# First keys of a fused attention and ELU kernel: a PSUM tile for each turned quarter, and two loads that change queues

## The chip, the cores and the metric

The kernel runs on one core of one Trainium2 chip. The metric is the device time of one execution in microseconds (us). A core has TensorE (PE, matmuls; PEld is its weight load), VectorE (DVE), ScalarE (ACT), GpSimd (POOL) and SyncE (SP). SP and ACT both issue DMAs here, each on a queue of its own: q1 in the profile is SP's, q10 is ACT's. All times below are us, those of the trace from the start of the span.

## The reference

Attention with a threshold, for 8 batches of 8 heads, 576 rows and 64 columns per head, then a feed-forward block with ELU over the 4608 rows of 512:

```python
scores = q @ k.T / 8                      # per batch and head, 576 x 576
thresh = max(scores, axis=-1) - tau
scores = where(scores >= thresh, scores, -1e9)
attn = exp(scores - max) / (sum + 1e-9)
x = attn @ v                              # heads side by side: 4608 x 512
h = x @ w_in                              # 512 -> 2048
out = where(h > 0, h, exp(min(h, 0)) - 1) @ w_out    # 2048 -> 512
```

## The kernel before

Attention goes pair of heads by pair of heads (32 pairs, two heads on 2 x 64 partitions), each pair in five steps of 128 query rows (the last of 64). Of a pair's queries and keys the kernel keeps `qT` and `kT`, with the 64 columns of a head on partitions and rows along the free axis. The scores of a step (`scores`, L681) are four matmuls: for each of two heads two halves of 288 keys. VectorE takes the row maximum (L738), a threshold is made of it (L756 or L742), ScalarE and VectorE make the masked exponentials (L761, L767, L776, L783), the weights are normalised, turned on TensorE or by VectorE, and multiplied with `v`. The feed-forward block of a batch is woven in on TensorE as soon as its rows are there, with a scheme of seven products in place of eight for most of the work. The order of all instructions on each engine is written out when the program is built, by a list of tasks with due times (`task`, `MOVED`); engines then run their own lists and wait for each other by semaphores.

The change is in the first of these tasks, `start()` in `early_tasks`, which runs once. It brings in the first pair's keys and the first 128 query rows, and turns them with TensorE. Loads, in the order of issue: on SP the keys of head 0 (`kb[:, 0]`, L1341), the keys of head 1 (`kb[:, 1]`, L1343), tau (L1345), the second 128 query rows of both heads (`qb[:, 1]`, L1346); on ACT the first query rows (`qb[:, 0]`, L1342) and the last 64 keys of both heads (`ends`, L1344). Behind them SP issues the loads of the next pair (L546), whose keys use the same tile `km` that holds `kb`.

A partition of `kb` holds four rows of a head's keys: they lie in two blocks of 128 columns (`e`), and a block holds two rows of 64 (`o`). TensorE turns one block at a time by a transposing matmul against the identity (`turn_rows`, L1357), and gets a 128 x 128 tile: on its first 64 partitions the quarter `o = 0`, on the others `o = 1`. Before, both blocks of a head lie in one PSUM tile (`a` for head 0, `b` for head 1), and for each `o` one copy (L1374) of 64 partitions by 256 columns brings two quarters into `kT`, one `o` by VectorE and the other by ScalarE. `ends` are turned into `turned[:, 1]` and copied by VectorE twice: `kT[:, S:]` (L1377), the tail of head 0's keys, and `kT[D:, :TAIL]` (L1378), that of head 1's. Head 0's keys stand in columns 64 to 640 of `kT`, head 1's in columns 0 to 576.

Ahead of the turns TensorE multiplies a constant tile (L1364) and then turns the identity eight times, to no use of the result (`warm`, L800), and once more before the turn of `ends`. The first step's four score matmuls have the heads one after the other (`HEADS_APART`): head 0 first half, head 0 second half, head 1 first half, head 1 second half. Then come, on TensorE, the turn of the second query rows (`rest_of_first_q`), which ScalarE copies (L1383), and the scores of the second step.

PSUM tiles: `blank` and `turned` are the two tiles of the pool `t` (four slots of 128 columns each, 2 KB per partition), `a`, `b`, `c` the three of the pool `s` (two banks each). Before, `c` is allotted here and not used.

Of the kernel before, what the change touches and what calls it, by code (L numbers as in the profile page):

```python
# [368 lines left out]
def kernel(  # L369
# [10 lines left out]
    nc = tc.nc  # L380
    PSUM = bass.MemoryType.PSUM
    P = 128
    B, H, S, D = q.shape
    DM, DF = moe_w_in.shape
    NC = S // P
# [930 lines left out]
    def early_tasks():  # L1316
# [18 lines left out]
        def start():  # L1335
            tiles = raws[0] = {"km": raw.tile([P, S // T, T], FP32, name="km")}
            kb = tiles["km"].rearrange("p j d -> p (j d)")[:, :MAIN].rearrange("p (i e f) -> p i e f", i=2, e=2)
            qb = wstage.tile([P, 2, 2, D], FP32, name="qb", bufs=1)
            ends = tiles["ends"] = wstage.tile([TAIL, 2, D], FP32, name="ends", bufs=1)

            nc.sync.dma_start(kb[:, 0], long_rows("k", 0).rearrange("p (e o) d -> p e (o d)", o=2))  # L1341
            nc.scalar.dma_start(qb[:, 0], first_rows("q", 0))  # L1342
            nc.sync.dma_start(kb[:, 1], long_rows("k", 1).rearrange("p (e o) d -> p e (o d)", o=2))  # L1343
            nc.scalar.dma_start(ends, first_rows("k", NC, TAIL))  # L1344
            nc.sync.dma_start(tau_sb, tau.to_broadcast([P, 1]))  # L1345
            nc.sync.dma_start(qb[:, 1], first_rows("q", 1))  # L1346
            nc.scalar.activation(keep, keep, AF.Exp)
            blank, turned = (psum["t"].tile([P, NC, P], FP32, name="rt", tag="rt") for _ in range(2))
            a, b, c = (psum["s"].tile([P, 2, 512], FP32, name="sc") for _ in range(3))
            qT, kT = room_q(0), room_k(0)  # L1350

            def warm(n):
                for _ in range(n):
                    transpose(blank[:, 0], ident)

            def turn_rows(dst, src, n=P):
                nc.tensor.matmul(dst, src, ident[:n, :n], is_transpose=True, skip_group_check=True)  # L1357

            def flat(src):
                return src.rearrange("p i d -> p (i d)")  # L1360

            ones = nc.const_aps.tensor(1.0, [P, P])
            for x in range(2):
                nc.tensor.matmul(blank[:, x], ones, ones, start=True, stop=True)  # L1364
            warm(8)
            turn_rows(turned[:, 0], flat(qb[:, 0]))
            nc.vector.tensor_copy(qT[:, :P], turned[:, 0])
            main = kT[:, TAIL:S].rearrange("p (e o n) -> p o e n", e=2, o=2)
            for h, room in ((0, a), (1, b)):
                r = slice(h * D, (h + 1) * D)  # L1370
                for e in range(2):
                    turn_rows(room[:, 0, e * P : (e + 1) * P], kb[:, h, e])
                for o, copy in ((h, nc.vector.tensor_copy), (1 - h, nc.scalar.copy)):
                    copy(main[r, o], room[o * D : (o + 1) * D, 0, : 2 * P].rearrange("p (e n) -> p e n", e=2))  # L1374
            warm(1)
            turn_rows(turned[:, 1, :TAIL], flat(ends), TAIL)
            nc.vector.tensor_copy(kT[:, S:], turned[:, 1, :TAIL])  # L1377
            nc.vector.tensor_copy(kT[D:, :TAIL], turned[D:, 1, :TAIL])  # L1378

            def rest_of_first_q():  # L1380
                rt = psum["t"].tile([P, NC, P], FP32, name="rt", tag="rt")
                turn_rows(rt[:, 0], flat(qb[:, 1]))
                nc.scalar.copy(qT[:, P : 2 * P], rt[:, 0])  # L1383

            first_q.append(rest_of_first_q)
            read_tau()
# [1019 lines left out]
```

## Time and profile before

| | |
|---|---|
| median of 3 runs | 1256.07 us (1256.03 to 1256.32) |
| profiled execution | 1257.65 us |
| its span in the trace | 1255.8 us |
| busy: PE, DVE, POOL, ACT | 1244.7, 1040.4, 727.8, 636.2 us |
| moved by DMA | 245.74 MB, mean 196 GB/s |

How to read the rows: a timeline row gives the start, the time taken, the engine, the line of the kernel, the operation, and "out<-in"; in brackets how long the engine stood idle before and what ended that. Rows with "x4" are merged: start of the first, sum of the stretch. "SPq" and "ACTq" rows are issues of DMAs by these engines. A row of a DMA issue group ends with its size and the time from the start of its issue to its landing. A row of a queue gives its packets and bytes up to the end of the window. A row of the chain of waits gives the start, the time and the line that the end of the kernel hung on. The ends of matmuls are modelled; their starts are not.

### The profile page before, as it was taken

To read this page: it belongs to the slowest core of one execution; us is meant where nothing else is said; L and a number is where in the kernel's file an instruction comes from. 1 tells how busy PE (TensorE), PEld (TensorE's weight loads), DVE (VectorE), ACT (ScalarE), POOL (GpSimd) and SP (SyncE) were. 2 spreads that over 40 slices of the span, in tenths; PEclk is the share of its full clock that TensorE was granted. 3 is DMA by queue.
4 is the path that set the end of the run, shared out by engine and by line. 5 is a ranking of instruction groups with operands and counts; after the bars stand their busy time and mean duration, and the time that the engine had idled before them with its cause. 6 is when DMAs were issued, how large, how long until landed. Compare 5 with 4: busy or idle time off the path is not lost.

```text
span 1255.8 us, 21112 instructions
## 1 busy us (share of the span) xinstructions
PE 1244.7 (99%) x6596; PEld 956.9 (76%) x6596; DVE 1040.4 (83%) x2196; ACT 636.2 (51%) x1334; POOL 727.8 (58%) x1064
## 2 busy tenths in 40 slices
PE   8999999999999999999999999999999999999998
PEld 6675576477887787878778787878788887788887
DVE  7888777789798978998889889898889876776983
ACT  7899776664453526253534445352625353465330
POOL 5778655687575748676576747584767655122000
PEclk9999999999999999999999999999999999999999
DMA  7456788998889998898989997999889885000001
GB/s 149 146 171 184 172 244 235 257 269 217 228 240 255 247 246 233 225 259 226 263 206 253 235 232 230 259 251 244 229 228 268 221 242 174 20 1 1 1 34 34
DMA packets 322303, 245.74 MB, mean 196 GB/s; under 512 B 205456, under 2 KB 286736, under 8 KB 322192
## 3 DMA queue, kind: packets, MB, share of 16 engines
q1 hardware_dynamic: 321376, 243.78, 72.3%
q8 instruction: 52, 0.85, 0.3%
q10 hardware_dynamic: 816, 0.62, 0.2%
q14 instruction: 59, 0.48, 0.2%
HBM read 154.53 MB, written 89.78 MB: 195 GB/s over the span
## 4 chain that ended last, share of the span: by engine, by line
PE 91%; DVE 3%; DMA 2%; ACT 2%; issue 1%; SPq 1%; POOL 1%; DVEq 0%; ACTq 0%; POOLq 0%
PE f L1869 23%; PE f L1729 21%; PE sc L985 8%; PE sc L1058 7%; PE f L2332 7%; PE f L2257 5%; PE f L1110 4%; PE sc L681 3%; PE f L1162 3%; PE f L2270 2%; PE pv L938 2%; PE rt L800 2%; PE sc L1050 1%; DMA there<-x 1%; PE sc L1045 1%
## 5 line engine op out<-in xcount | busy, mean ns | idle before, releaser
L992 DVE TENSOR_REDUCE mx<-sc 128x1 f32<-128x576 f32 x207 | 148.3, 750 | 30.0 <-PE sc L985 26.1
L734 POOL TENSOR_SCALAR w<-w,rs 128x576 f32<-128x576 f32 x144 | 115.8, 813 | 69.6 <-DVE rs L797 69.5
L1012 ACT ACTIVATE w<-sc,mx 128x576 f32<-128x576 f32 x113 | 81.5, 740 | 115.6 <-DVE mx L992 98.7
L876 DVE STREAM_TRANSPOSE x<-w 128x512 f32<-128x512 f32 (+1 forms) x153 | 108.9, 744 | 12.9 <-POOL w L734 11.5
L1004 POOL TENSOR_SCALAR th<-mx,ntau 128x2 f32<-128x2 f32 (+1 forms) x114 | 33.8, 296 | 134.5 <-DVE mx L992 134.5
L985 PE MATMUL sc<-kT,qT 64*128 64x448 f32 (+4 forms) x736 | 103.1, 416 | 0.2 <-ACT xs L1074 0.2
L985 PEld LDWEIGHTS sc<-kT,qT 64*128 64x128 f32 x736 | 80.7, 186 | 25.2 <-issue 16.2
L1019 DVE SCALAR_TENSOR_TENSOR w<-sc,th,w 128x576 f32<-128x576 f32 x113 | 88.2, 810 | 9.4 <-ACT w L1012 9.2
L1729 PE MATMUL f<-xt,sw 128*128 128x256 f32 x384 | 93.4, 386 | 0.4 <-DVE g L1751 0.4
L1729 PE MATMUL f<-xt,w_in 128*128 128x256 f32 x384 | 92.3, 382 | 0.0
L1869 PE MATMUL f<-w_out,s 128*128 128x256 f32 x384 | 92.0, 382 | 0.1
L1869 PE MATMUL f<-w_out,g 128*128 128x256 f32 x384 | 92.0, 382 | 0.0
L1729 PE MATMUL f<-x,w_in 128*128 128x256 f32 x384 | 90.9, 379 | 0.1
L1869 PE MATMUL f<-t,s 128*128 128x256 f32 x384 | 90.8, 379 | 0.0
L734 POOL TENSOR_SCALAR e<-e,rs 128x576 f32<-128x576 f32 x91 | 67.1, 741 | 35.3 <-DVE rs L797 33.9
L1729 PEld LDWEIGHTS f<-xt,sw 128*128 128x128 f32 x384 | 69.5, 189 | 16.7 <-issue 5.4
L1729 PEld LDWEIGHTS f<-xt,w_in 128*128 128x128 f32 x384 | 71.7, 190 | 12.8 <-ACT w L1743 2.2
L1869 PEld LDWEIGHTS f<-w_out,g 128*128 128x128 f32 x384 | 72.0, 190 | 12.4 <-issue 3.1
L1869 PEld LDWEIGHTS f<-w_out,s 128*128 128x128 f32 x384 | 71.9, 190 | 12.4 <-issue 2.5
L1729 PEld LDWEIGHTS f<-x,w_in 128*128 128x128 f32 x384 | 72.8, 190 | 10.5 <-ACT s L1743 0.7
L1869 PEld LDWEIGHTS f<-t,s 128*128 128x128 f32 x384 | 72.8, 190 | 10.3 <-POOL s L1816 0.4
L1816 POOL TENSOR_TENSOR s<-g 128x256 f32<-128x256 f32 x96 | 74.9, 785 | 8.0 <-DVE g L1779 7.5
(330 smaller groups left out, 3106.3 us busy)
## 6 DMA issues: line engine op xcount, KB each, us to landing
there<-x SPq DMA_DIRECT2D x444, 144.0 KB, 3.5
wTb<-there SPq DMA_DIRECT2D x58, 576.0 KB, 6.4
wTa<-there SPq DMA_DIRECT2D x53, 576.0 KB, 4.8
sw<-win_sums SPq DMA_DIRECT2D x46, 384.0 KB, 4.5
t<-wout_sums SPq DMA_DIRECT2D x33, 512.0 KB, 6.2
qm<-in_q_dram SPq DMA_DIRECT2D x124, 72.0 KB, 4.9
wst<-in_moe_w_in_dram SPq DMA_DIRECT2D x16, 512.0 KB, 4.5
vm<-in_v_dram SPq DMA_DIRECT2D x64, 128.0 KB, 3.8
```

Source lines behind the costliest of these rows:

```text
L734: nc.gpsimd.tensor_scalar(wv, wv, st["rs"][:, h : h + 1], 1.0, ALU.mult, ALU.mult)
L876: nc.vector.transpose(x[:, :, c0 : c0 + nc_], src.rearrange("p (c g n) -> p g c n", c=nc_, n=T))
L985: on_banks(nc.tensor.matmul(o, qT[r, i * P : (i + 1) * P], kT[r, k0 : k0 + n], start=True, stop=True, skip_group_check=True), o)
L992: on_banks(nc.vector.tensor_reduce(st["mx"][:, h : h + 1], st["sc", h], axis=AX.XY if i == NC else AX.X, op=ALU.max, negate=True), st["sc" ...
L1012: on_banks(nc.scalar.activation(st["e", h], st["sc", h], AF.Exp, bias=st["mx"][:, h : h + 1]), st["sc", h])
L1019: on_banks(nc.vector.scalar_tensor_tensor(st["e", h], st["sc", h], st["th"][:, h : h + 1], st["e", h], ALU.is_ge, ALU.mult, accum_out=st[" ...
L1058: on_banks(nc.tensor.matmul(o, vm[:, h, c], parts[part][:, g0:g1, h * (NC + 1) + c], start=False, stop=(c == NC - 1), skip_group_check=Tru ...
L1729: nc.tensor.matmul(loc["banks"][place], left[:, j], right[:, j], start=(begins and j == 0), stop=(j == 1), skip_group_check=True)
L1816: engine.tensor_tensor(o, x, y, op)
L1869: nc.tensor.matmul(place(m), lhs, rhs, start=(begins and v == 0), stop=(v == RU - 1), skip_group_check=True)
L2257: nc.tensor.matmul(o, w.rearrange("p (j f) -> p j f", j=KJ)[:, j], m, start=(j == 0 and x == 0), stop=(j == KJ - 1 and x == 1), skip_group ...
L2332: nc.tensor.matmul(banks8[2 * i + x // 2], h[:, tok], w, start=(f == 0 and x != 1), stop=(f == NFT - 1 and x != 0), skip_group_check=True)
```

## The change

Three things change in `start()`. The loads of head 1's keys and of the last keys change places: the last keys are SP's second load, head 1's keys ACT's second. Each block of turned keys gets a PSUM tile of its own: head 0's blocks `a` and `b`, head 1's `c` and the second slot of `blank`. VectorE copies both quarters of block 0 and ScalarE both quarters of block 1, each quarter by a copy of 64 partitions by 128 columns. And the order on TensorE becomes: six turns of the identity, head 0's two blocks, the first query rows, one turn of the identity, head 1's two blocks, the last keys. On VectorE the two copies of head 0 come ahead of that of the queries, and those of head 1 ahead of the two copies of the last keys. The order of all that follows on every engine is the same as before.

```diff
             nc.sync.dma_start(kb[:, 0], long_rows("k", 0).rearrange("p (e o) d -> p e (o d)", o=2))
             nc.scalar.dma_start(qb[:, 0], first_rows("q", 0))
-            nc.sync.dma_start(kb[:, 1], long_rows("k", 1).rearrange("p (e o) d -> p e (o d)", o=2))
-            nc.scalar.dma_start(ends, first_rows("k", NC, TAIL))
+            nc.sync.dma_start(ends, first_rows("k", NC, TAIL))
+            nc.scalar.dma_start(kb[:, 1], long_rows("k", 1).rearrange("p (e o) d -> p e (o d)", o=2))
             nc.sync.dma_start(tau_sb, tau.to_broadcast([P, 1]))
             nc.sync.dma_start(qb[:, 1], first_rows("q", 1))
...
-            warm(8)
+            def turn_keys(h, rooms):
+                for e in range(2):
+                    turn_rows(rooms[e], kb[:, h, e])
+
+            def copy_keys(h, rooms):
+                for e, copy in ((0, nc.vector.tensor_copy), (1, nc.scalar.copy)):
+                    for o in range(2):
+                        k0 = TAIL + (2 * e + o) * P
+                        copy(kT[h * D : (h + 1) * D, k0 : k0 + P], rooms[e][o * D : (o + 1) * D])
+
+            warm(6)
+            sides = (a[:, 0, :P], b[:, 0, :P]), (c[:, 0, :P], blank[:, 1])
+            turn_keys(0, sides[0])
             turn_rows(turned[:, 0], flat(qb[:, 0]))
+            copy_keys(0, sides[0])
             nc.vector.tensor_copy(qT[:, :P], turned[:, 0])
-            main = kT[:, TAIL:S].rearrange("p (e o n) -> p o e n", e=2, o=2)
-            for h, room in ((0, a), (1, b)):
-                r = slice(h * D, (h + 1) * D)
-                for e in range(2):
-                    turn_rows(room[:, 0, e * P : (e + 1) * P], kb[:, h, e])
-                for o, copy in ((h, nc.vector.tensor_copy), (1 - h, nc.scalar.copy)):
-                    copy(main[r, o], room[o * D : (o + 1) * D, 0, : 2 * P].rearrange("p (e n) -> p e n", e=2))
             warm(1)
+            turn_keys(1, sides[1])
             turn_rows(turned[:, 1, :TAIL], flat(ends), TAIL)
+            copy_keys(1, sides[1])
             nc.vector.tensor_copy(kT[:, S:], turned[:, 1, :TAIL])
             nc.vector.tensor_copy(kT[D:, :TAIL], turned[D:, 1, :TAIL])
```

## The prediction

> **What bounds the kernel now.** I read the page first, then the chain of waits for the first 20 us, then the timeline of each engine up to 11 us, then the DMA issues and queues of the same stretch.
>
> ```profile
> span 1255.8 us, 21112 instructions
> PE 1244.7 (99%) x6596; PEld 956.9 (76%) x6596; DVE 1040.4 (83%) x2196; ACT 636.2 (51%) x1334; POOL 727.8 (58%) x1064
> PE 91%; DVE 3%; DMA 2%; ACT 2%; issue 1%; SPq 1%; POOL 1%; DVEq 0%; ACTq 0%; POOLq 0%
> ```
>
> TensorE holds 91% of the chain that ended last. Nothing after the start is edited, so what the edit can give is a shift of the start that all later work carries along. The size of that shift is decided before 9 us:
>
> ```profile
> 3.87 0.85 PE sc L1357 x4
> 5.23 1.38 PE sc L681 x4
> 6.64 0.77 DVE mx L738
> 7.78 0.67 DVE mx L738
> 8.79 0.02 ACT w L761
> ```
>
> The chain runs through the four key turns (L1357), the first scores (L681), the two row maxima of VectorE, and into ScalarE's softmax. I call the four score matmuls of the first tile S1, S2 (head 0, first and second half of the keys), S3, S4 (head 1). The handle for the sum is the start of the first maximum, 6.64, which needs S2, and ScalarE's two L761, which need the maxima and stand behind the copy of the next queries.
>
> ```profile
> 1.53 1.72 PEld L800 LDWEIGHTS rt<-ident 128*128 128x128 f32 x8
> 3.32 0.18 PEld L1357 LDWEIGHTS rt<-ident,qb 128*128 128x128 f32 x1
> 3.45 0.42 PE L1357 MATMUL rt<-ident,qb 128*128 128x128 f32 x1
> 3.66 1.06 PE L1357 MATMUL sc<-ident,km 128*128 128x128 f32 x4
> 4.87 0.37 PE L1357 MATMUL rt<-ident,ends 64*128 64x64 f32 x1
> 5.21 1.44 PEld L681 LDWEIGHTS sc<-x 64*128 64x128 f32 x8 [0.16 <-ACT x L1374]
> 7.04 0.33 PE L1357 MATMUL rt<-ident,qb 128*128 128x128 f32 x1
> 5.21 0.91 PE L681 MATMUL sc<-x 64*128 64x288 f32 x2
> 5.71 0.67 PE L681 MATMUL sc<-x 64*128 64x288 f32 x3
> 6.20 0.42 PE L681 MATMUL sc<-x 64*128 64x288 f32 x2
> ```
>
> The last three rows are from narrow windows: S1's two passes start at 5.21 and 5.71, half a microsecond apart, and S2's second pass starts at 6.20, so from 5.71 a pass takes (6.20 - 5.71) / 2 = 0.245. A turn of 128 columns takes (3.66 - 3.45) = 0.21 here.
>
> ```profile
> 3.91 0.29 DVE L1367 COPY x<-rt 128x128 f32<-128x128 f32 x1 [2.93 <-PE rt L1357]
> 4.33 0.42 DVE L1374 COPY x<-sc 64x256 f32<-64x256 f32 x1
> 4.78 0.43 DVE L1374 COPY x<-sc 64x256 f32<-64x256 f32 x1
> 5.27 0.23 DVE L1377 COPY x<-rt 128x64 f32<-128x64 f32 x1
> 5.53 0.23 DVE L1378 COPY x<-rt 64x64 f32<-64x64 f32 x1
> 4.79 0.82 ACT L1374 COPY x<-sc 64x256 f32<-64x256 f32 x2 [1.30 <-DVE x L1374]
> 7.41 0.27 ACT L1383 COPY x<-rt 128x128 f32<-128x128 f32 x1 [1.80 <-PE rt L1357]
> 7.82 1.80 ACT L761 ACTIVATE w<-sc,th,keep 128x576 f32<-128x576 f32 x2
> 6.32 0.19 POOL L444 TENSOR_SCALAR ntau<-floor 128x1 f32<-128x1 f32 x1
> ```
>
> The point the edit attacks is the row of ScalarE at 4.79: it waits 1.30 us, the end of it for VectorE's copy of the other half of the same PSUM tile (4.33 to 4.75). Its first copy ends near 5.16 (half of 0.82 after 4.79, less the gap), and S1 starts at 5.21. A copy follows its turn by 3.91 - 3.45 = 0.46.
>
> **The parts of the change.**
>
> *The turns move ahead, two warm-ups go.* The query turn stood at 3.32 because its load lands then, not because the warm-ups ended (1.53 + 1.72 = 3.25):
>
> ```profile
> km<-in_k_dram SPq DMA_DIRECT2D x1, 128.0 KB, 2.3
> qb<-in_q_dram ACTq DMA_DIRECT2D x1, 64.0 KB, 2.6
> ends<-in_k_dram ACTq DMA_DIRECT2D x1, 32.0 KB, 3.3
> km<-in_k_dram SPq DMA_DIRECT2D x1, 128.0 KB, 2.4
> 0.72 0.48 ACTq L1342 DMA_DIRECT2D qb<-in_q_dram  x1
> 1.17 0.42 SPq L1343 DMA_DIRECT2D km<-in_k_dram  x1
> 1.23 0.73 ACTq L1344 DMA_DIRECT2D ends<-in_k_dram  x1
> ```
>
> Queries: 0.72 + 2.6 = 3.32. The keys of head 0 are issued at the same 0.72 on the other queue and land at 0.72 + 2.3 = 3.02; six warm-ups end at 1.53 + 6 x 0.215 = 2.82. So head 0's turns can start at 3.02 (weights) and 3.15 (matmul), against 3.66 now: 0.5 us earlier. The query turn comes third, at 3.58, one warm-up later TensorE is free at 4.0.
>
> *ScalarE and VectorE copy at once, in four copies per engine instead of two.* A 64x128 copy is not in the trace; it lies between the 0.23 of 64 columns and the 0.42 of 256 columns. I take 0.29, the row of 128 columns (L1367), with 0.02 between. VectorE's row then is: head 0's first quarters 3.61 (3.15 + 0.46) to 3.92 and to 4.23, query copy to 4.54. ScalarE, free of its table load by 3.6, copies the other quarters of head 0 from 3.82 to 4.45. Both are done 0.6 to 0.7 us before the 5.16 of now. But VectorE has 4 x 0.29 in place of 2 x 0.42, 0.3 us more, ahead of the tail copies (now L1377, L1378) for which S2 and S3 wait. Its earliest finish: head 1's two quarters 4.56 to 5.16, first tail copy 5.18 to 5.41, second to 5.66, against 5.50 and 5.76 now. That row alone leaves a gain of 0.1 at the tail copies; the half microsecond from the turns is mostly spent there.
>
> *Head 1's keys go second on ScalarE's queue, the tail second on SP's.* This is the dear part. Now head 1's keys land at 1.17 + 2.4 = 3.57. Second on the other queue, at 1.23, the only transfer in the trace is the tail: 1.23 + 3.3 = 4.53. The first one there took 2.6, so the bounds are 1.23 + 2.6 = 3.83 and 4.53, with more possible because it has four times the bytes (128 against 32 KB). What the queues moved up to 2.9 and up to 3.9 us (q10 is ScalarE's):
>
> ```profile
> q1 hardware_dynamic: 257, 0.24, 28.1%
> q10 hardware_dynamic: 299, 0.07, 11.2%
> q1 hardware_dynamic: 550, 0.30, 28.3%
> q10 hardware_dynamic: 398, 0.09, 10.9%
> ```
>
> Between 2.9 and 3.9 q10 moved 99 packets and q1 293: the second transfer of q10 dribbled while the bytes were few, so it is not bytes that delay it, and four times the bytes need not cost four times. I take the middle, 4.2 (an estimate from these two bounds). TensorE then stands idle from 4.0 to 4.2; turned are head 1's quarters at 4.33 and 4.54, the tail at 4.75. S1 starts at about 4.92 (5.21 now), its second pass at 5.42. VectorE: head 1's quarters 4.79 to 5.39, tail copies to 5.64 and 5.89. S2 may start 0.15 behind the first of these (as S3 does now behind L1378: 5.76 and 0.15 make 5.91), 5.79; TensorE is free of S1 at about 5.80, if passes become quick at 5.7 as now. S2's second pass then begins at 6.04, and the maximum 0.44 behind it (now 6.20 to 6.64), at 6.48: 0.16 earlier. S3 and S4 start at 6.04 instead of 5.90, so the turn of the next queries (7.04 now) moves to 7.18 and ScalarE's copy of them (7.41) to 7.55, done at 7.82. L761's first, 7.82 now, is therefore not earlier, but the second is held by its maximum, and comes 0.1 earlier. TensorE's next scores, behind that copy, are 0.14 later, but their maxima have VectorE's work ahead of them. Sum: -0.1 us. The threshold that VectorE computes between the maxima needs POOL's constants, ready at 6.51, and the first maximum ends no earlier than 7.2: that cover holds.
>
> Each 0.1 us by which the load lands later moves all of this by 0.1: no change at 4.3, +0.15 at 4.53, +0.4 at 4.8.
>
> *Other queues.* SP's loads of the next keys reuse the tile and wait for the turns of head 1:
>
> ```profile
> 4.96 2.03 SPq L546 DMA_DIRECT2D km<-in_k_dram  x4
> 12.24 0.74 DVE L592 STREAM_TRANSPOSE x<-km 128x576 f32<-128x576 f32 x1
> ```
>
> They are issued by 6.99 and used at 12.24; half a microsecond more is covered by the two or three us between landing and use. If that cover were gone it would cost the same half microsecond. The tail's load, now on SP, has the slot in which keys took 2.4, so it is there by 4.5 even at its present 3.3; all orders after that are the same.
>
> **The sum.** The profiled execution took 1257.65 us (span 1255.8), 1.58 above the median of the runs shown, 1256.07. The sum is a difference, 1257.65 - 0.1 = 1257.55, and on the median it gives 1255.97, say 1256.0. For a measurement of this kernel 0.2% is 2.5 us; the whole edited stretch, from first load to first maximum, is 6.6 us and no term in it is over 1 us.
>
> **The rivals.**
>
> *Faster: the load is not late.* If head 1's keys share the engines evenly from 2.9 on, 392 packets a microsecond in the rows above give 196 to q10, the 128 packets and their completions need 0.7 us, and with 0.15 to be seen they are there at 3.75. Then VectorE's row is the bound (first tail copy done at 5.41), S1 starts at 4.8, S2 at 5.73, the maximum at 6.41: -0.2 us, 1255.85. For it speaks that 1 KB rows landed fast on SP; against it that q10 had 99 of 392 packets, a quarter. [...]
>
> *Slower: the load lands like the tail or later.* From 4.3 on it decides: at 4.53 TensorE idles half a microsecond, VectorE's four remaining copies start at 5.12, S2 at 6.1, +0.15; at 4.8, +0.4. 1256.2 to 1256.5. For it speaks the only row of that slot, 3.3; against it that its 0.73 of issue belongs to 256-byte pieces, where 1 KB rows took 0.42.
>
> *Slower: the quick passes come later.* S1's first pass took 0.5, every pass after 5.71 0.245. What makes them quick at 5.7 the trace doesn't say; before that TensorE was busy nearly without gap from 0.76. The changed kernel puts a gap of 0.2 to 0.5 at 4.0 and drops two of eight warm-ups. If the change of pace then falls behind S4, S1 to S4 and the next scores run at 0.5 a pass: S2's second pass at 6.4, the maximum near 7.1, S4 behind 7.5, the query turn near 8.05, its copy to 8.8, and L761 a full microsecond late: +1.0, 1257.1. It decides as soon as the gap is what counts. [...]
>
> *No shift:* the change at the start is swallowed by a later wait, e.g. on a load; 1256.07. It lies inside the first case.
>
> **How the numbers follow.** Forecast (load at 3.9 to 4.4, -0.2 to +0.05): 0.5. Faster rival: 0.17. Late load: 0.2. Late pace: 0.1. Something in the later 1250 us that answers to small shifts by more than themselves: 0.03. Later work may add or take some 0.4 us in each case, since 1250 us of engines and loads stand against each other in a new phase (the runs shown spread over 0.3). The range reaches from 1255.85 - 0.5 to 1256.5 + 0.35: 1255.3 to 1256.9; outside are the late pace and half the rest. Only that rest reaches 2.5 us: faster 0.01, slower 0.02, within 0.97.
>
> **What would show it.** Right: head 0's first turn near 3.15, ScalarE's copies no longer behind VectorE's, an idle TensorE of 0.1 to 0.4 before head 1's first turn, VectorE's second tail copy done near 5.9, the maximum near 6.5. Head 1's load landing before 3.9 or after 4.5 shows the size of that term wrong; a pass of 0.5 after 5.8 shows the late pace. Wrong altogether: a first maximum within these bounds and a time off by over 1 us, for then the start does not set the end.

## The result, and the profile after

The changed kernel takes 1259.74 us (median of 8 runs, 1258.69 to 1262.4), the kernel before 1256.12 beside it (8 runs, 1255.97 to 1256.4): the ratio is 1.0029, 95% interval 1.002 to 1.0039. It is 3.6 us slower, where 0.1 us faster was forecast, with a range of 1255.3 to 1256.9; a change of 2.5 us to the slower side had been given a chance of 0.02. The profiled execution took 1258.86 us, its span 1257.0.

The start did what was asked of it, and more. From the timeline and the DMA issues of the changed kernel (a row gives start, time taken, engine, line):

```profile
3.08 0.29 PEld L1357 LDWEIGHTS sc<-ident,km 128*128 128x128 f32 x2 [0.24 <-DMA km<-in_k_dram]
3.83 0.18 PEld L1357 LDWEIGHTS sc<-ident,km 128*128 128x128 f32 x1
3.80 0.54 ACT L1373 COPY x<-sc 64x128 f32<-64x128 f32 x2 [0.56 <-PE sc L1357]
4.53 0.59 DVE L1373 COPY x<-sc 64x128 f32<-64x128 f32 x2
5.41 0.23 DVE L1386 COPY x<-rt 64x64 f32<-64x64 f32 x1
6.29 0.76 DVE L738 TENSOR_REDUCE mx<-sc 128x1 f32<-128x576 f32 x1 [0.65 <-PE sc L681]
...
km<-in_k_dram ACTq DMA_DIRECT2D x1, 128.0 KB, 2.5
1.24 0.48 ACTq L1344 DMA_DIRECT2D km<-in_k_dram  x1
```

ScalarE's copies stand behind their turn alone, not behind VectorE. Head 1's keys land at 1.24 + 2.5 = 3.74, and their turn follows at 3.83 with no idle time ahead of it. The first maximum stands at 6.29, 0.35 us earlier than the 6.64 of before. VectorE keeps this 0.35, but for a stretch near 9 us, until 25 us. Then it is lost and more, within 3 us. First the timeline of the kernel before in that stretch, then that of the changed kernel:

```profile
26.09 0.82 DVE L783 SCALAR_TENSOR_TENSOR w<-sc,th,e 128x576 f32<-128x576 f32 x1
27.34 0.52 DVE L717 TENSOR_SCALAR w<-w,rs 128x576 f32<-128x576 f32 x1
27.55 1.47 POOL L502 TENSOR_TENSOR wtop<-wtop,wst 128x512 int32<-128x512 int32 x1 [1.11 <-ACT wst L487]
28.01 0.63 PE L800 MATMUL rt<-ident,w 128*128 128x128 f32 x4 [0.28 <-DVE w L717]
```

```profile
26.05 0.82 DVE L783 SCALAR_TENSOR_TENSOR w<-sc,th,e 128x576 f32<-128x576 f32 x1 [0.23 <-issue]
27.30 1.50 DVE L717 TENSOR_SCALAR w<-w,rs 128x576 f32<-128x576 f32 x1
27.20 1.28 POOL L502 TENSOR_TENSOR wtop<-wtop,wst 128x512 int32<-128x512 int32 x1 [1.13 <-ACT wst L487]
28.95 1.09 PE L800 MATMUL rt<-ident,w 128*128 128x128 f32 x4 [1.58 <-DVE w L717]
```

The windows of both, before first (a row: span of the window, its length, busy time of PE, PEld, DVE, ACT and POOL, the granted clock):

```profile
28.90:32.20 3.30, 3.30 (x27) 2.11 (x28) 3.25 (x8) 3.27 (x6) 0.86 (x4) 1.00 0.90 244
```

```profile
25.40:28.80 3.40, 1.97 (x9) 0.93 (x9) 3.06 (x8) 2.60 (x6) 1.96 (x2) 1.00 0.69 108
28.90:32.20 3.30, 3.25 (x14) 2.06 (x16) 3.30 (x7) 2.12 (x4) 0.76 (x3) 0.50 0.99 259
32.30:36.00 3.70, 3.70 (x32) 2.45 (x29) 1.75 (x6) 2.00 (x5) 1.47 (x2) 1.00 0.69 193
```

And the same scores in the chain of waits, before and after:

```profile
31.54 1.22 PE sc L681 x8
```

```profile
34.04 1.22 PE sc L681 x8
```

Three steps can be read here.

1. **A loss of 0.23 us** stands ahead of the second L783: "issue" means that VectorE waited for nothing that the profile shows. This row had no idle time before. Of the 0.35 only 0.04 is left (26.05 against 26.09).
2. **A collision.** GpSimd gets its data from ScalarE as much earlier as all else (L502 at 27.20 against 27.55), but VectorE's L717 does not (27.30 against 27.34). Before, L717 started 0.21 ahead of L502 and took 0.52. Now it starts 0.10 behind it, and takes 1.50: L502 ends at 27.20 + 1.28 = 28.48, and L717 0.32 behind it, at 28.80. TensorE, which needs its result, stands idle 1.58 in place of 0.28 and is 0.94 late.
3. **The clock.** TensorE was busy for 1.97 us of the 3.40 up to 28.80. Then its granted clock (the share of full speed that the trace records) is 0.50, in the trace from 28.83 to 32.25, 3.41 us. The next scores of the chain stand at 34.04 against 31.54: 2.50 late.

From there the shift stays at 2.5 to 2.6 us until 571, where it falls to 1.2, the difference of the two spans. That is a wait in the profiled execution of before, not a gain of the change. The chain of waits of before, then of the changed kernel, in that stretch:

```profile
549.73 6.61 DMA there<-x
556.36 7.87 DMA wTb<-there
564.27 0.47 PE sc L1050 x2
```

```profile
553.12 12.38 PE f L1737 x56
565.50 0.40 PE sc L1045 x2
```

Before hung on two DMAs there, in this execution; the changed kernel runs through. The kernel before with one instruction added, told of below, makes the same step: its shift against this trace falls from 0.28 to -1.18 at 570 us, and its profiled execution took 1256.46. So the wait belongs to this execution, and is worth 1.4 of the 1.58 by which it was above the median. A second trace of the changed kernel (`again` below) hangs on the same two DMAs there and loses 0.9. The shift of 2.6, not the 1.2 of the two spans, is the profiled loss of the changed kernel: 1258.86 - 1256.12 is 2.7.

The times that follow lie in two heaps some 2 us apart for each kernel, the one before too, so that a lowest time or a count at times says more than a median. The twenty traces tell why: the granted clock is full from 3.6 to 5.7 us on in eight of them and from 12.8 to 13.9 on in nine, and in three it comes at 4.3 to 4.7, falls at 7.7 to 8.1 and is back at 14.5 to 15.0.

### The profile page after: what moved, and what is told of

The parts are those of the page before. It is cut to its first block, busy times and chain, and to the rows that moved or that the text cites. A ratio compares the mean times of both kernels' runs of the same rounds, so it can differ in the third digit from the quotient of the medians.

```text
span 1257.0 us, 21113 instructions
## 1 busy us (share of the span) xinstructions
PE 1245.3 (99%) x6594; PEld 957.0 (76%) x6594; DVE 1041.6 (83%) x2198; ACT 635.9 (51%) x1336; POOL 727.7 (58%) x1064
## 4 chain that ended last, share of the span: by engine, by line
PE 92%; DVE 3%; DMA 2%; ACT 1%; issue 1%; SPq 1%; POOL 1%; DVEq 0%; ACTq 0%; POOLq 0%
PE f L1877 23%; PE f L1737 23%; PE sc L985 8%; PE sc L1058 7%; PE f L2340 7%; PE f L2265 5%; PE f L1110 4%; PE sc L681 3%; PE f L1162 3%; PE f L2278 2%; PE pv L938 2%; PE rt L800 2%; PE sc L1050 1%; DMA there<-x 1%; PE sc L1045 1%
## 5 line engine op out<-in xcount | busy, mean ns | idle before, releaser
L876 DVE STREAM_TRANSPOSE x<-w 128x512 f32<-128x512 f32 (+1 forms) x153 | 108.9, 744 | 13.1 <-POOL w L734 11.7
L1737 PEld LDWEIGHTS f<-xt,w_in 128*128 128x128 f32 x384 | 71.7, 190 | 12.8 <-ACT w L1751 2.2
```

Of the source, the lines that this page charges most:

```text
L876: nc.vector.transpose(x[:, :, c0 : c0 + nc_], src.rearrange("p (c g n) -> p g c n", c=nc_, n=T))
L1737: nc.tensor.matmul(loc["banks"][place], left[:, j], right[:, j], start=(begins and j == 0), stop=(j == 1), skip_group_check=True)
```

## Experiments

**The theory** after the first look: the two instructions that VectorE's list got longer by (four copies of keys in place of two, with the same two of the tail, all ahead of the first maximum) put another instruction at a place of that list where a few tenths are lost, and there it shows; L717 then misses its turn before L502. **The rivals:** the start's earlier phase, the exchange of the loads, or the gap in TensorE's work makes the loss.

### The change again, and the two list entries alone

The first kernel is the changed one unaltered. The second is the kernel before with this:

```diff
     nc.vector.memset(qds[0], 0.0)
+    nc.vector.memset(qds[0][:, :1], 0.0), nc.vector.memset(qds[0][:, :1], 0.0)
```

> The changed kernel once more, for a second profile. In its first trace the start came out 0.35 us earlier (first maximum at 6.29, not 6.64), then VectorE's L717 took 1.50 us instead of 0.52 because GpSimd's L502 had started ahead of it (27.20 against 27.30), TensorE stood idle 1.9 us before 28.95, and the granted clock was 0.5 from 28.8 to 32.2: from there all is 2.5 us late. Theory A (port order: this collision is the cause of all of it) expects the same collision in this trace, the first maximum at 6.29 +- 0.05, and 1258.7 to 1262.4. Rival B (chance: a clock that lapses here and there, the collision only in that one execution) expects a trace with L717 at 0.52 and lapses elsewhere, or none.

> The kernel before with two more tiny VectorE memsets at its start, in VectorE's idle time, so that VectorE's list is as much longer as in the changed kernel, and nothing else is moved. In the changed kernel's trace VectorE lost 0.23 us for no shown reason ahead of its second L783 (26.05), and only by that it came behind GpSimd. Theory C (the two instructions more on VectorE's list make that loss, by where its instructions are fetched) expects the loss here too, near 26.1, the collision at 27.4, and 1257.5 to 1262. Rival D (the 0.35 us shift of the start against something that didn't shift makes it) expects 1256.1 +- 0.3 and L717 at 0.52.

The changed kernel again took 1259.27 (1257.17 to 1261.86, 9 runs), ratio 1.0022, interval 1.0012 to 1.0032, with the same loss, 0.24, and L717 at 1.49 behind L502. But the clock does not fall after it in this trace: its full clock came late, at 13.19. (The idle TensorE of 1.9 us in the expectation is counted from the start of the matmul ahead of it; the row says 1.58.) The kernel before with two tiny instructions took 1259.09 (1257.25 to 1260.88), ratio 1.002, interval 1.001 to 1.0029. Its timeline (lines are one further down):

```profile
28.18 0.82 DVE L784 SCALAR_TENSOR_TENSOR w<-sc,th,e 128x576 f32<-128x576 f32 x1 [0.21 <-issue]
29.43 1.52 DVE L718 TENSOR_SCALAR w<-w,rs 128x576 f32<-128x576 f32 x1
29.35 1.28 POOL L503 TENSOR_TENSOR wtop<-wtop,wst 128x512 int32<-128x512 int32 x1 [1.12 <-ACT wst L488]
```

```profile
30.70:34.00 3.30, 2.91 (x12) 1.91 (x14) 3.30 (x6) 1.78 (x4) 0.77 (x3) 0.50 0.91 229
```

Loss, collision and half clock are all there, without one of the three edits. Two entries on a list, 0.18 us of work at a time when VectorE had nothing to do, cost the 3 us.

### Other phase of the start

The changed kernel with two warm-ups back:

```diff
-            warm(6)
+            warm(8)
```

> The changed kernel with eight warm-up turns instead of six: the list on VectorE is the changed one, the start some 0.2 us later than the changed kernel's, first maximum at 6.4 to 6.6. Theory C (length of VectorE's list) expects the collision and 1258 to 1262. Rival D (the shift) expects it gone or lessened, 1255.8 to 1256.5.

1259.23 (1257.56 to 1259.83), ratio 1.0019, interval 1.0009 to 1.0028. The first maximum comes only 0.04 earlier than before, and the loss (0.22) and L717 (1.50) stand in its trace unchanged. It is not the earlier phase that makes them.

And the loads exchanged back, all else changed:

```diff
-            nc.sync.dma_start(ends, first_rows("k", NC, TAIL))
-            nc.scalar.dma_start(kb[:, 1], long_rows("k", 1).rearrange("p (e o) d -> p e (o d)", o=2))
+            nc.sync.dma_start(kb[:, 1], long_rows("k", 1).rearrange("p (e o) d -> p e (o d)", o=2))
+            nc.scalar.dma_start(ends, first_rows("k", NC, TAIL))
```

> The changed kernel with the two loads in their old places, for the start alone: head 1's keys second on SP, the tail second on ScalarE's queue. If the exchange of the loads is dear, as the prediction had it, head 1's first turn is earlier or the first maximum is earlier than 6.29; if it is what makes the gain, the tail's turn waits for its load until 4.8 and the first maximum is at 6.5 or later. With VectorE's list as long as in the changed kernel, theory C expects the collision here too: L717 at 1.5.

1260.4 in one run; the same loss (0.22) and L717 of 1.50. The first maximum stands at 6.17, 0.47 earlier than before: the exchange of the loads is neither the price nor the gain.

### The length of VectorE's list

The kernel before with one and with four of the tiny instructions at the start, and the changed kernel with two instructions given to other engines, so that the list is as long as before:

```diff
-    nc.vector.memset(qds[0], 0.0)
+    nc.gpsimd.memset(qds[0], 0.0)
...
-            nc.vector.tensor_copy(kT[D:, :TAIL], turned[D:, 1, :TAIL])
+            nc.scalar.copy(kT[D:, :TAIL], turned[D:, 1, :TAIL])
```

> The kernel before with one tiny memset more on VectorE's list. With two more, VectorE lost 0.21 us ahead of the second L783. If what counts is which instruction stands at one certain place of the list, one more puts the sum (L791) there; the loss of 0.2 then falls one instruction later or vanishes in its wait: theory C expects either the same collision (loss of 0.2 anywhere between L783 and L717 is enough, 1258 to 1260.5) or no loss at all (1256.1); rival D expects 1256.1.

> The same with four more. Theory C: the place then falls on an instruction two earlier than in the changed kernel, the wait of VectorE for ScalarE's exponentials (0.73 us idle), which would hide it: 1256.1 to 1256.5, L717 at 0.52. If instead any longer list makes the loss, 1258 to 1260.5.

> The changed kernel with two instructions moved off VectorE's list: the first clearing of a tile goes to GpSimd, the second tail copy to ScalarE, so that VectorE's list is as long as before the change. Theory C (the two instructions more on VectorE's list make the loss of 0.23 us near 26 us, and by it the collision of L717 with GpSimd's L502) expects the loss gone, L717 at 0.5 to 0.6, no lapse of the clock near 29, and the earlier start kept: 0.35 us under the kernel before, 1255.8 where the clock is released near 5 us, with the same second heap some 2 us higher as the kernel before (released near 13 us: 1257.8). Rival D (the shift of the start makes the collision) expects the collision as in the changed kernel and 1258.7 to 1260.

One more: 1256.61 (1256.46 to 1258.42), ratio 0.9996, interval 0.9987 to 1.0005. Four more: 1257.12 (1255.9 to 1258.65), 1.0004, interval 0.9995 to 1.0013. The changed kernel with the old length: 1256.32 (1255.9 to 1258.08), 0.9996, interval 0.9986 to 1.0006. None has the loss, and L717 is 0.52 in each. Two medians are above what was expected, and not for the loss: with four more, five of ten executions lie in the upper heap, and with one more the lower heap itself starts at 1256.46, which was not followed up. Of the last:

```profile
27.65 0.81 DVE L783 SCALAR_TENSOR_TENSOR w<-sc,th,e 128x576 f32<-128x576 f32 x1
28.90 0.52 DVE L717 TENSOR_SCALAR w<-w,rs 128x576 f32<-128x576 f32 x1
29.11 1.46 POOL L502 TENSOR_TENSOR wtop<-wtop,wst 128x512 int32<-128x512 int32 x1 [1.11 <-ACT wst L487]
```

It is not the number of instructions that costs, since four cost nothing, but two exactly. Between none and two, the changed kernel with only the second tail copy moved to ScalarE (one more than before), and between two and four, the changed kernel with one tiny instruction added:

> The changed kernel with only the second tail copy moved to ScalarE: VectorE's list is one longer than before the change. After one more instruction on the list of the kernel before, nothing was lost. Theory C (the place in the list counts) expects no loss, no collision, the start 0.35 us early, and 1255.8 to 1256.2 for the runs with an early release of the clock, 2 us more for the late ones; under the kernel before by 0.2 to 0.4 in each heap. Rival D (the shift) expects 1258.7 to 1260.

> The changed kernel as it is, with one tiny useless VectorE instruction more at the very start (a memset of one column), so that VectorE's list is three longer than before in place of two. Nothing is taken away. Theory (a certain place on VectorE's list costs a few tenths, and with exactly two more it is the instruction right ahead of L717 that stands there): the loss before the second L783 goes or is hidden, L717 takes 0.52 again ahead of GpSimd's L502, and the time falls to 1255.9 to 1256.7 in most runs. Rival (each further instruction on VectorE is a further burden, or the new order of the start is what costs): 1258.7 to 1260, at least the time of the changed kernel.

One more: 1258.09 (1256.16 to 1259.88, 11 runs), ratio 1.0009, interval 1.0 to 1.0017. Three more: 1257.74 (1256.11 to 1260.11, 11 runs), ratio 1.001, interval 1.0002 to 1.0019. In both traces the loss is gone and L717 takes 0.52. The lowest times, 1256.16 and 1256.11, are those of the kernel before, while the lowest of the changed kernel in 17 runs is 1257.17. So one useless instruction added to the changed kernel takes away what two had brought. But nine and eight of the eleven executions lie in the upper heap: the median with one more is that of the late executions in its expectation, and the one with three more is above the 1255.9 to 1256.7 expected of most. That is a second matter, taken up below.

### Where on the list

Two tiny instructions in the kernel before, put in elsewhere: `nc.vector.memset(floor, 0.0)` twice, behind the turn of the other queries, behind the first L717, and behind the first L592.

> The kernel before with two tiny useless VectorE instructions (memsets of one column) behind VectorE's turn of the other queries of the first pair (about 12 us in), in place of the start. Theory (the place on VectorE's list counts, wherever the two are put in ahead of it): the same loss of 0.2 to 0.3 before the second L783, L717 1.5 long behind GpSimd's L502, 1258.3 to 1259.5. Rival (a start with two more instructions on VectorE is another start, and what follows comes from there): no loss, L717 0.52, 1256.0 to 1256.7.

> The kernel before with two tiny useless VectorE instructions (memsets of one column) right behind the first L717, so behind the place where the loss lay. Theory (only what comes ahead of that place moves it): no loss before the second L783, the first L717 0.52 long, 1256.0 to 1256.8. Rival (two more instructions on VectorE cost the same wherever they stand, by their number): 1258.3 to 1259.5.

> The kernel before with two tiny useless VectorE instructions (memsets of one column) behind the first L592, at about 13 us: ahead of the place of the loss, and with 1 us of idle VectorE between them and it. (The last such kernel had its two at 36 us, behind the place, and so tested the other side.) Theory (it is the place on the list that counts): the loss of 0.2 to 0.3 before the second L783 at 26 us, the L717 behind it 1.5 long behind GpSimd's L502, 1258.3 to 1259.5. Rival (two more at the very start make another start): no loss, L717 0.52, 1256.0 to 1256.8.

The first went in at 36 us and not at 12, I had misread where that turn stands; so it lies behind the place, as the second does (27.66). They took 1256.14 (1255.79 to 1257.97), ratio 1.0002, interval 0.9993 to 1.0011, and 1256.87 (1255.74 to 1258.18), 1.0005, interval 0.9996 to 1.0014, without the loss. The third, at 14.7 us in this execution, has the loss and the collision, 1259.38 (1257.51 to 1261.05), ratio 1.002, interval 1.001 to 1.0029; its full clock came at 13.05 and does not fall after the collision:

```profile
14.71 0.19 DVE L594 MEMSET floor<- 128x1 f32 x2
28.16 0.82 DVE L785 SCALAR_TENSOR_TENSOR w<-sc,th,e 128x576 f32<-128x576 f32 x1 [0.22 <-issue]
29.41 1.51 DVE L719 TENSOR_SCALAR w<-w,rs 128x576 f32<-128x576 f32 x1
29.32 1.28 POOL L502 TENSOR_TENSOR wtop<-wtop,wst 128x512 int32<-128x512 int32 x1 [1.12 <-ACT wst L487]
```

So it is the place: two entries ahead of it, wherever they stand, and none behind it. In all ten traces with the loss, the second L783 is the 64th record (row of the trace) of VectorE, its semaphore waits counted. In the kernel before, a short reduction (L791) is the 64th and nothing is seen to be lost. What happens at that place is not settled, and I found no such loss at other multiples of 64 or 128 in the traces. One candidate, which no run tested, is the loading of instructions: in all twenty traces the first 8 KB packet after the start on the queue that the page calls `q14 instruction` begins 0.2 to 1.1 us behind VectorE's 64th record, with the loss and without. The trace doesn't say which engine it is for, and it begins only after the loss (27.13 against 26.05 in the changed kernel), so the loss is not a wait for this packet.

### The collision

Four edits at the changed kernel. L717 of that step given to ScalarE (`ACT_NORM` gets `(4, 0)`, `NORM_DVE` loses it); GpSimd's two steps L494 and L502 one task later (`"add_1"` from 11.1 to 13.1); L502 of that piece in two halves; and eight useless turns in the gap that L717 leaves on TensorE (`IDLES` gets `(4, 0, 8)`). The third:

```diff
-            nc.gpsimd.tensor_tensor(top, top, staged[i][:, :, 0].bitcast(I32), ALU.add)
+            for cols in (slice(0, WN // 2), slice(WN // 2, WN)) if i == 1 else (slice(0, WN),):
+                nc.gpsimd.tensor_tensor(top[:, cols], top[:, cols], staged[i][:, cols, 0].bitcast(I32), ALU.add)
```

> The changed kernel with the one multiplication that collides (L717 of the fifth step, head 0) given to ScalarE (L722), VectorE's and GpSimd's lists as they are otherwise. Theory A (the collision carries the loss; the 0.23 alone is nearly free) expects no 1.5 us instruction near 27.3, no lapse at 28.8, and 1255.8 to 1256.6 with the clock released early. If the loss of 0.23 or something else in the changed start carries it, 1257.5 or more stays.

> The changed kernel with GpSimd's two conversions of the second weight piece (L494, L502) behind one more threshold (L742) of the next step, which waits for VectorE's maximum behind L717: they can no longer start ahead of L717. All else, VectorE's list too, is as changed. Theory A (the collision carries the loss) expects the 0.2 us loss ahead of the second L783 still there, L717 back at 0.5 to 0.6, no long idle TensorE near 28 and no lapse of the clock there; 1255.8 to 1256.5 with the clock released early, some 2 us more with it released late. If the lost 0.2 carries the loss by itself, 1258 or more stays.

> The changed kernel with the conversion that collides (L502 of the second weight piece, 1.28 us) made in two halves of 256 columns. Theory A, as a dose: VectorE's L717 then waits for one half at most, takes 0.8 to 1.2 us instead of 1.5, and TensorE's gap shrinks by 0.3 to 0.7; the total falls by at least that, to 1256.5 to 1258.5, as the lapse of the clock gets rarer. If L717's time has nothing to do with GpSimd's instruction, it stays at 1.5.

> The changed kernel with eight useless turns of the identity on TensorE (0.9 us) in the place where it stood idle 1.9 us, behind 27.04 and ahead of the turn of the weights that waits for L717. If the lapse of the clock there is a second cause on top of the collision, the half clock is gone, L717 still takes 1.5, and the time falls by the 1.5 us that the half clock cost: 1257.2 +- 0.5, with a much smaller spread. If the lapse is not caused by that gap, the time stays at 1258.7 to 1262.

The loss stays in all four (0.21 to 0.24), as it should.

The first was no clean test: 1259.78 (1257.53 to 1262.17), ratio 1.0024, interval 1.0014 to 1.0034, where 1255.8 to 1256.6 was expected. On ScalarE the step stands ahead of the copies that TensorE waits for, TensorE is idle 1.27 behind them, and the clock falls at 31.59.

The second brings L717 back to 0.52, but GpSimd's threshold now waits behind these two steps, and VectorE loses 1.00 there at 33.51: 1259.16 (1257.04 to 1260.23), ratio 1.0011, interval 1.0002 to 1.0021. The delay was moved, not removed.

The third has a median near that of before. Its timeline, the two halves in rows of their own:

```profile
29.37 0.94 DVE L718 TENSOR_SCALAR w<-w,rs 128x576 f32<-128x576 f32 x1
29.26 0.73 POOL L503 TENSOR_TENSOR wtop<-wtop,wst 128x256 int32<-128x256 int32 x1 [1.13 <-ACT wst L487]
29.95 0.95 POOL L503 TENSOR_TENSOR wtop<-wtop,wst 128x256 int32<-128x256 int32 x1
```

L717 now takes 0.94, between 0.52 and 1.50: it ends 0.32 behind the first half (29.26 + 0.73 = 29.99), as it ended 0.32 behind the whole before. The time is 1256.82 (1256.42 to 1261.13), ratio 1.0004, interval 0.9995 to 1.0013. With the loss still in, as the profile shows it, most of the 3 us has gone from the median: the loss counts mainly by what it makes VectorE miss. The profiled execution is not one of those, though: it took 1261.13, the longest of the ten, with a full clock only from 13.48 on and a fall from 30.54 to 33.96. So the trace shows the shorter L717, and the times of the others, without a trace, the smaller price. In every trace in which the two overlap, the one that starts second is longer: with L717 0.20 to 0.22 ahead (ten traces) it takes 0.52 and L502 1.45 to 1.47; with L717 0.08 to 0.11 behind (seven traces) L502 takes 1.28 to 1.30 and L717 1.49 to 1.52, and behind the half of 0.73 it takes 0.94. What the one holds from the other, a port as the name of theory A has it, no trace shows.

The fourth: 1259.23 (1257.17 to 1260.32), ratio 1.0013, interval 1.0004 to 1.0022, where 1257.2 with half a microsecond of play was expected. In its trace the collision is there (L717 1.51) and the clock does not fall after it. By itself that shows little, as the clock doesn't fall in two traces with the collision and an unfilled gap either (`again` and the two instructions at 14.7). What tells these apart is how the gap lies. In every trace the stretches between two changes of the granted clock are whole multiples of 3.413 us (23.89 is seven of them, 17.07 five). Divided so, the piece with the least work of TensorE near 30 us is this, in the changed kernel, in `again` and with the two at 14.7 (the first number after the length is PE's busy time):

```profile
25.42:28.83 3.41, 1.95 (x9) 0.91 (x8) 3.08 (x8) 2.58 (x6) 1.94 (x2) 1.00 0.68 107
26.85:30.26 3.41, 2.53 (x14) 1.32 (x11) 2.91 (x7) 3.06 (x7) 2.29 (x3) 1.00 0.72 117
30.11:33.53 3.42, 2.46 (x20) 1.73 (x22) 3.42 (x6) 2.13 (x4) 1.02 (x3) 1.00 0.84 211
```

Ahead of all six falls near 30 us the piece has 1.84 to 2.39 us of work; in the four traces with the loss and no fall the least is 2.46. Where the pieces begin differs by execution, so the same gap can lie in one of them or be shared by two.

The times of the traces split the price. Without the loss, five with an early clock took 1256.07 to 1256.95 (the sixth is the profile of before, with its wait at 550), the four with a late or twice lost one 1257.99 to 1258.33. With the collision, a late clock and no fall it is 1259.22, 1259.36, and 1260.08 in `again`, of which 0.9 is its wait at 573. With the fall it is 1258.86 and 1259.15 where the clock came early, 1260.88 where it came late. So the collision costs about 1.1, the fall about 1.6 and a late clock about 2; these are estimates from so few executions.

### Does the start's gain live to the end?

The changed kernel with the list as long as before, in more rounds; and the same with two useless turns in TensorE's gap ahead of the second scores:

```diff
                 turn_rows(rt[:, 0], flat(qb[:, 1]))
+                for _ in range(2):
+                    transpose(turned[:, 0], ident)
```

> The changed kernel with VectorE's list as long as before (the first memset by GpSimd, the second copy of the last keys by ScalarE), as run already, in more rounds: does it beat the kernel before? Theory (the start's gain of 0.35 us, less a tenth or so, lives to the end): early runs at 1255.9 to 1256.0 against 1256.1 to 1256.3, so a median 0.2 to 0.3 lower and a ratio of 0.9998. Rival (the gain is eaten by a later wait, as at 571 us in other runs): both at 1256.1 to 1256.2.

> The changed kernel with VectorE's list as long as before, and two useless turns of the identity on TensorE behind the turn of the second query rows, in the gap of 0.35 us ahead of the second scores. Of the four kernels with the new start and without the loss 27 of 43 executions took over 1257.5, of the kernel before and its variants without the loss 56 of 168. Theory (with the new start TensorE's busy stretch around 5 to 9 us is thinner, so more executions get the full clock late or lose it at 8 us again; this gap is part of it): a third or fewer above 1257.5, median at 1256.0, below the kernel before by 0.1 to 0.3. Rival (the gap that decides is another, such as that ahead of head 1's turns or those between the first scores): still some six in ten above 1257.5, median at 1257.7.

The first took 1257.66 (1255.75 to 1258.67, 11 runs), ratio 1.0008, interval 0.9999 to 1.0017, where 0.9998 was expected. Its lowest three, 1255.75 to 1255.81, are some 0.2 below most of the lower heap of before in the same runs (1255.9 to 1256.06). But the lowest of before there is 1255.78, and that of the kernel with two instructions behind the place 1255.74. So it is not shown that the start's gain lives to the end, at 0.2 or at all. And six of eleven took over 1257.5. Its scores, and the same in the second kernel, whose clock came early:

```profile
5.01 3.16 PE L681 MATMUL sc<-x 64*128 64x288 f32 x8
8.93 3.02 PE L681 MATMUL sc<-x 64*128 64x288 f32 x8 [0.36 <-ACT x L1391]
```

```profile
6.96 0.38 PE L800 MATMUL rt<-ident 128*128 128x128 f32 x2
7.48 2.06 PE L681 MATMUL sc<-x 64*128 64x288 f32 x8
```

Eight passes in 3.02 are slow ones, in 2.06 quick ones. In the three-more kernel above it went the third way, which three of the thirteen traces with the new start took and none of the seven with the old: quick from 4.7, then a granted clock of 0.50 again:

```profile
5.00:8.00 3.00, 2.54 (x11) 1.39 (x10) 2.17 (x6) 0.90 (x3) 1.04 (x5) 1.00 0.86 139
8.20:14.90 6.70, 6.70 (x27) 5.57 (x26) 4.71 (x12) 5.18 (x11) 2.78 (x6) 0.50 0.62 152
```

Of the kernels with the new start and without the loss, 27 of 43 executions took over 1257.5; of the kernel before and its variants without the loss, 56 of 168. That is about twice as often, which at 2 us would be 0.6 us on a mean, more than the start gains. Set by set it is less clear: beside the kernel before in the same runs it is 4 of 10 against 13 of 30, 9 of 11 against 13 of 27, and 14 of 22 against 8 of 33. With the gap filled, 4 of 11 did, against 6 of 20 of before beside it: 1256.75 (1255.95 to 1258.11), ratio 1.0003, interval 0.9994 to 1.0012. The median expected was 1256.0, below that of before; it is above it (1256.35). So it is not shown that the thinner work of TensorE at 5 to 9 us is the reason; eleven executions are too few to tell 4 from the 6 of eleven without the filling.

No kernel that was run beats the one before by more than its interval.

## Why the prediction was wrong

**What held.** Head 0's turns at 3.08 to 3.24 (3.02 and 3.15 predicted), the 64x128 copies at 0.29 (two in 0.59), ScalarE no longer behind VectorE, VectorE's row as the bound of the start.

**A term of wrong size.** The load of head 1's keys was put at 4.2, between 3.83 and 4.53, because the only transfer known in that slot, the tail, took 3.3. It landed at 3.74, outside both bounds. The rival "the load is not late" had 3.75, and its sum, a maximum at 6.41, is near the 6.29 measured; the forecast had 6.48. The even shares of the engines that this rival supposed are not in the trace: from 2.4 to 3.0 q10 moved 331 packets and q1 33. The tail's 3.3 belonged to the tail and not to the slot: in that slot the keys took 2.5, and in the other queue's second slot the tail took 2.8 where keys had taken 2.4. Why the tail takes longer with a quarter of the bytes, no run shows. This error made the start 0.2 us faster than forecast; it did not make the time longer.

**The step that failed** is the second sentence on the bound: nothing after the start is edited, so the edit can only give a shift. The order of all later instructions is unchanged, but not their place on VectorE's list, and the part on the four copies counted their 0.3 us and not that they are two entries more. Two such entries alone, put into the kernel before, took 1259.09, and the changed kernel with two instructions taken off that list 1256.32: they make VectorE lose 0.23, by which L717 comes behind L502 and takes 1.50 in place of 0.52, and the half clock can follow. The sum had no term for it; "something in the later 1250 us that answers to small shifts by more than themselves" had 0.03, and was no mechanism. The signs were in the trace of before: L717 stood 0.21 ahead of L502, so that a slip of VectorE against GpSimd by more than that would put the longer L502 first (it was 0.31), and 0.28 of TensorE's idle time hung on L717. I didn't look for such narrow orders between VectorE and GpSimd. What I could not have read there is the loss itself: its place shows in no row of before.

**The late pace** was a real thing and not a matter of this kernel alone. It comes by execution, in both kernels, and costs about 2, where 1.0 was predicted; neither the three runs of before then shown nor the eight beside the result had it. After the collision the half clock also comes at 30 us, a place where the prediction saw no danger. In the profiled execution the full clock came at 4.94, so the loss read there is not this rival's.

**The sum as measured,** in the profiled execution: -0.35 at the start, +0.31 by the loss (L783 would have started with the record ahead of it, at 25.74, as the two do before at 26.09), to -0.04; +0.98 by the collision, to +0.94; +1.56 in the stretch of the half clock, to +2.50; and 0.1 in the rest. The median of all executions is 3.6 above. That the difference is executions with a late or twice lost clock fits the times of the later traces; seven of the eight executions of the result have no trace, so for them it is not shown. Why VectorE loses the 0.23 at that place is open.

## What to carry to other kernels

The few tenths gained at this start were more than lost when two instructions that overlap changed their order (L717 took 0.52 ahead of L502 and 1.50 behind it): look through the trace for pairs on VectorE and GpSimd that start within a few tenths of each other, and ask which comes first after the change. When a kernel gets slower with all edited rows as planned, walk the shift of one engine along the whole trace and stop at the first jump; then put the suspected cost alone, with no use, into the kernel before. An instruction added has a place as well as a duration: two memsets in the kernel before gave 1259.09 and 1259.38 ahead of the place on VectorE's list, 1256.14 and 1256.87 behind it.

## What the runs showed of the hardware

- VectorE loses 0.21 to 0.24 us ahead of the second L783, a 576-column instruction, in all ten traces in which it is VectorE's 64th record. In the ten others a short reduction, a read of a sum or a wait has that place, and nothing is seen to be lost. It is the same with the two extra instructions at the start or 14.7 us in; the reason is open.
- TensorE's clock fell to 0.50 for 3.41 us after 3.40 us in which it was busy for 1.97. The longest gap of that stretch, which ran on to 28.95, was 1.58: no idle time as long as the 3.41 stood ahead of the fall. Near 30 us the six pieces of 3.413 us ahead of a fall were busy for 1.84 to 2.39, and pieces of 2.46 and more had no fall behind them. At 8 us it is not so simple: the clock fell behind pieces of 2.90 to 2.95 in three traces, and not behind one of 2.79 (the kernel before with two instructions behind L717).
- Two executions of one kernel differ by some 2 us with the time at which the quick passes begin: without the loss the traces with an early clock took 1256.07 to 1256.95 (but for the wait of before at 550), those with a late or twice lost one 1257.99 to 1258.33. The changed kernel's two traces have the full clock from 4.94 and from 13.19. Whether the edit of the start changed how often it comes late is not settled (4 of 10, 9 of 11 and 14 of 22 against 13 of 30, 13 of 27 and 8 of 33).
